# A gate h·cos(h) on one core: the range reduction of the sine without its absolute value

## The chip, the core and the metric

The kernel runs on one core of a Trainium2 chip. The core has a matrix engine (TensorE, PE in the profile), a vector engine (VectorE, DVE), a scalar engine for activation functions (ScalarE, ACT), GpSimd (POOL), and queues that move data by DMA; each has its own stream of instructions and they wait for each other by semaphores. The metric is the device time of one execution in microseconds (us), as the median of several runs.

## The reference

A small attention block makes 4352 rows of 512 numbers; a feed-forward block with a gate follows. All is float32.

```python
def _attn_ref(x, state):          # x (8, 8, 512, 64), state (8, 8, 32, 64)
    scores = scale * np.matmul(x, state.transpose(0, 1, 3, 2))
    ...                           # softmax over the last axis -> a
    xread = np.matmul(a, state)
    scores2 = scale * np.matmul(state, x.transpose(0, 1, 3, 2))
    ...                           # softmax -> a2
    sread = np.matmul(a2, x)
    return np.concatenate([xread, sread], axis=2)

def _moe_ref(x, w_in, w_out):     # x (4352, 512), w_in (512, 2048), w_out (2048, 512)
    h = x @ w_in
    g = h * np.cos(h)
    return g @ w_out
```

The change concerns `g = h * np.cos(h)`.

## The kernel before

The hidden values h are made transposed, in tiles of 128 hidden units by 512 tokens, 16 for each of the 8 batches, and 16 more tiles of 256 columns for the state rows: 144 tiles. The kernel keeps h in turns (h / 2π), so the factor of the sine is 2π. A tile passes five steps after its matmuls: two on ScalarE and one on VectorE that bring the angle into the range of the sine, the sine itself on ScalarE, and the product on VectorE. The constant 12582912 is 1.5·2^23: adding it to a small float32 rounds that to an integer, and subtracting it again gives the integer. The cosine of h turns is then sin(π/2 − 2π·|n − h|), n being that integer; the absolute value keeps the argument between −π/2 and π/2.

```python
MAGIC = 12582912.0
TWO_PI = 2.0 * math.pi
...
msb = ctx.enter_context(tc.tile_pool(name="msb", bufs=2))          # q
hps = ctx.enter_context(tc.tile_pool(name="hps", bufs=2, space=PSUM))  # h
ctx.enter_context(tc.manual_schedule())     # each engine runs in the order written
...
def hidden(t):
    t.hp = hps.tile([P, S], F32, name="h")[:, 0:t.n]
    for i in range(t.kn):
        nc.tensor.matmul(out=t.hp, lhsT=t.lhs(i), rhs=t.rhs(i),
                         start=(i == 0), stop=(i == t.kn - 1))      # L467

def gate(t):
    t.q = msb.tile([P, S], F32, name="q")[:, 0:t.n]
    nc.scalar.activation(t.q, t.hp, func=ACTF.Copy, bias=MAGIC)     # L473

def gate2(t):
    nc.vector.scalar_tensor_tensor(out=t.q, in0=t.q, scalar=MAGIC,  # L476
                                   in1=t.hp, op0=ALU.subtract,
                                   op1=ALU.subtract)

def gate3(t):
    nc.scalar.activation(t.q, t.q, func=ACTF.Abs)                   # L481
    nc.scalar.activation(t.q, t.q, func=ACTF.Sin, bias=halfpi,      # L482
                         scale=-TWO_PI)

def gate4(t):
    t.slot = g_free.pop(0)
    t.g = g_all[:, t.slot, 0:t.n]
    nc.vector.tensor_tensor(t.g, t.hp, t.q, op=ALU.mult)            # L488
```

The loop over the tiles mixes the gate with other work, and that order is the order of each engine:

```python
for step, t in enumerate(all_tiles):
    ...
    hidden(t)
    go(0)                      # PE: parts of the next batch's attention
    gate(t)
    gate2(t)
    go(1); go(3)               # ACT and DVE: parts of the next batch's attention
    convert(last, "bcdf")      # DVE, POOL: weights of an earlier step, bit work
    convert(conv, "1")         # ACT: weights (in some steps after gate4)
    gate3(t)
    later.pop(0)()             # DVE: an output transposed for storing, if there is one
    gate4(t)
    sums(t)                    # DVE or POOL: sums of g tiles
    go(2)
    convert(conv, "2")         # ACT
    go(4)
    ...
    while len(line) >= (LAG if step >= 2 * NH else LAG + 1):
        output(line.pop(0))    # PE: products of g with w_out, LAG = 3 tiles later (L532)
    line.append(t)
```

The weights come in a form whose exponent and mantissa are put together on the chip in parts: `convert` is two passes on ScalarE (L225, L228), two on VectorE (L231, L234) and one on GpSimd (L239) for each piece, in the first 15 steps or so. `products` (L314) multiplies a piece of w_in with a batch's states into `sw`, which ScalarE or VectorE copies to SBUF (L441). The attention's softmax uses the exponential on ScalarE (L355, L360) and a row of VectorE operations (L328 to L381); before the exponentials of a batch, and before the next sine, ScalarE loads another table of functions. `warm` (L709) are matmuls of zeros that keep PE going in the first steps.

## Time and profile before

| | |
|---|---|
| time, median of 3 runs | 787.93 us (786.89 to 788.06) |
| span of the profiled run | 785.0 us |
| PE matmul busy | 765.1 us |
| VectorE busy | 417.3 us |
| ScalarE busy | 389.1 us |
| GpSimd busy | 176.7 us |
| TensorE clock granted | full speed throughout |

The span falls into three stages. In the table each cell is busy time in us in that stage; DMA is the mean share of the 16 DMA engines.

| stage (us from the start) | PE | DVE | ACT | POOL | DMA |
|---|---|---|---|---|---|
| 41 to 103: weights are still converted | 54.46 | 46.23 | 56.98 | 24.31 | 0.64 |
| 103 to 160: last conversions, batch 2 is prepared | 54.17 | 39.24 | 30.88 | 44.65 | 0.20 |
| 160 to 785: steady work, and the state rows at the end | 619.29 | 305.18 | 276.53 | 94.93 | 0.19 |

Busy time counts an instruction from its start to its end. PE's matmuls overlap each other, so a busy PE isn't PE at its peak; the spacing of their starts tells more. In a row of the profile's groups stand the line of the kernel, the engine, the operation, the tile written and the tile read, their shapes, how often, the busy time and the mean time of one, and after the second bar the time for which the engine stood idle just before, with what ended it. L473 means line 473.

### The profile page before, as it was taken

The page shows a single profiled execution, that of the slowest core. Times are in us where ns is not written, and L with a number is a line of the kernel's source. Part 1 is how long each engine was busy: PE and PEld are TensorE (multiplying, and loading weights), DVE is VectorE, ACT ScalarE, POOL GpSimd, SP SyncE. Part 2 cuts the span into 40 slices and gives each one's busy share as a digit, 9 for nine tenths or more (in the row PEclk, how much of TensorE's full clock was granted, in tenths as well). Part 3 has the DMA queues.
Part 4 walks back from the last instruction along what each step waited for, and adds up shares of the span by engine and source line. Part 5 has one row for each costly group of instructions (what it writes and reads, how often), then busy time and mean ns, then how long its engine had stood idle before and what let it go on. Part 6 is the DMA issues. An engine that isn't in the chain of part 4 may idle for free.

```text
span 785.0 us, 7535 instructions
## 1 busy us (share of the span) xinstructions
PE 765.1 (97%) x2664; PEld 340.3 (43%) x2664; DVE 417.3 (53%) x656; ACT 389.1 (50%) x626; POOL 176.7 (23%) x118
## 2 busy tenths in 40 slices
PE   8998899899999999999999999999999999999997
PEld 3443433344344444444344434434444444455554
DVE  5768778623563466734554467635554446431431
ACT  3888954733463545633473446443563445322222
POOL 2344359673000000641000001640000004610200
PEclk9999999999999999999999999999999999999999
DMA  8595451060011510250104310330100114000021
GB/s 241 167 263 187 141 100 28 4 104 1 3 25 31 102 24 5 34 101 0 24 5 76 58 27 15 54 67 0 28 1 0 28 28 130 4 0 15 13 41 40
DMA packets 161957, 43.49 MB, mean 55 GB/s; under 512 B 153920, under 2 KB 153920, under 8 KB 161920
## 3 DMA queue, kind: packets, MB, share of 16 engines
q1 hardware_dynamic: 161024, 42.49, 24.8%
q10 hardware_dynamic: 768, 0.39, 0.2%
q8 instruction: 21, 0.34, 0.2%
q0 software_dynamic: 128, 0.13, 0.1%
q14 instruction: 16, 0.13, 0.1%
HBM read 34.08 MB, written 8.91 MB: 55 GB/s over the span
## 4 chain that ended last, share of the span: by engine, by line
PE 81%; ACT 10%; DVE 6%; issue 1%; DMA 1%; SPq 0%; POOL 0%; DVEq 0%
PE o L532 44%; PE h L467 26%; PE at L314 4%; PE o L652 4%; PE at L404 2%; ACT q L482 1%; ACT q L481 1%; ACT s L228 1%; DVE q L476 1%; ACT q L473 1%; DVE g_all L488 1%; ACT xT L360 1%; ACT w_in L225 1%; ACT L482 1%; DVE xT L334 1%
## 5 line engine op out<-in xcount | busy, mean ns | idle before, releaser
L467 PE MATMUL h<-aT,sw 128*128 128x512 f32 x512 | 241.5, 594 | 11.0 <-DVE g_all L488 8.1
L532 PE MATMUL o<-g_all,w_out 128*128 128x512 f32 x512 | 236.4, 598 | 1.2 <-POOL w_out L239 1.2
L494 POOL TENSOR_TENSOR g_all<-g_all 128x512 f32<-128x512 f32 x80 | 112.1, 1423 | 451.5 <-DVE g_all L488 447.9
L473 ACT ACTIVATE q<-h 128x512 f32<-128x512 f32 (+1 forms) x144 | 82.1, 570 | 262.3 <-PE h L467 262.2
L476 DVE SCALAR_TENSOR_TENSOR q<-q,h 128x512 f32<-128x512 f32 (+1 forms) x144 | 94.2, 654 | 216.9 <-ACT q L473 216.9
L532 PE MATMUL o<-g_all,s 128*128 128x512 f32 x384 | 177.3, 598 | 0.0
L488 DVE TENSOR_TENSOR g_all<-h,q 128x512 f32<-128x512 f32 (+1 forms) x144 | 94.8, 658 | 124.8 <-ACT q L482 118.6
L467 PEld LDWEIGHTS h<-aT,sw 128*128 128x128 f32 x512 | 96.4, 190 | 135.4 <-issue 110.7
L532 PEld LDWEIGHTS o<-g_all,w_out 128*128 128x128 f32 x512 | 94.0, 190 | 125.5 <-issue 118.4
L481 ACT ACTIVATE q<-q 128x512 f32<-128x512 f32 (+1 forms) x144 | 87.6, 608 | 93.5 <-DVE q L476 93.4
L532 PEld LDWEIGHTS o<-g_all,s 128*128 128x128 f32 x384 | 70.8, 190 | 91.7 <-issue 87.3
L482 ACT ACTIVATE q<-q,halfpi 128x512 f32<-128x512 f32 (+1 forms) x144 | 100.5, 698 | 4.5
L239 POOL TENSOR_TENSOR w_out<-w_out,s 128x1024 int32<-128x1024 int32 x10 | 23.9, 2390 | 77.1 <-DVE w_out L234 73.5
L494 DVE TENSOR_TENSOR g_all<-g_all 128x512 f32<-128x512 f32 x48 | 33.2, 692 | 1.6
L441 ACT COPY sw<-at 128x512 f32<-128x512 f32 x50 | 26.8, 589 | 9.0 <-PE at L314 9.0
L467 PE MATMUL h<-sT,w_in 128*128 128x256 f32 x128 | 30.2, 379 | 0.0
L652 PE MATMUL o<-w_out,g_all 128*128 128x512 f32 x64 | 29.6, 592 | 0.0
L467 PEld LDWEIGHTS h<-sT,w_in 128*128 128x128 f32 x128 | 24.3, 190 | 10.1 <-issue 6.7
L239 POOL TENSOR_TENSOR w_in<-w_in,s 128x1024 int32<-128x1024 int32 (+1 forms) x10 | 19.3, 1929 | 38.8 <-DVE w_in L234 36.5
L314 PE MATMUL at<-w_in,stT 64*32 64x512 f32 x400 | 27.2, 601 | 0.0
L538 DVE SCALAR_TENSOR_TENSOR held<-o,held 128x512 f32<-128x512 f32 x40 | 25.3, 675 | 2.9 <-PE o L532 2.9
L559 DVE STREAM_TRANSPOSE ot<-held 128x512 f32<-128x512 f32 x32 | 22.1, 692 | 0.0
(80 smaller groups left out, 427.7 us busy)
## 6 DMA issues: line engine op xcount, KB each, us to landing
out_dram<-ot SPq DMA_DIRECT2D x132, 64.0 KB, 2.0
g_all<-in_moe_w_out_dram SPq DMA_DIRECT2D x8, 1024.0 KB, 4.9
g_all<-in_moe_w_in_dram SPq DMA_DIRECT2D x6, 1024.0 KB, 5.2
xT<-in_x_dram SPq DMA_DIRECT2D x96, 64.0 KB, 2.3
x_b<-in_x_dram SPq DMA_DIRECT2D x24, 256.0 KB, 4.6
x_b<-in_x_dram SPq DMA_DIRECT2D x16, 128.0 KB, 4.0
g_all<-in_moe_w_in_dram SPq DMA_DIRECT2D x4, 512.0 KB, 6.0
x_b<-in_moe_w_out_dram SPq DMA_DIRECT2D x1, 1024.0 KB, 5.9
```

Source lines behind the costliest of these rows:

```text
L239: nc.gpsimd.tensor_tensor(bits, bits, e, op=ALU.add)
L314: nc.tensor.matmul(out=(to or at)[j][Ns * k:Ns * k + Ns, 0:n], lhsT=w[D * j:D * j + D, self.b, Ns * k:Ns * k + Ns], rhs=r(slice(D * j, D * ...
L441: (copy or nc.scalar.copy)(sw_of[self.b, nt][:, j, c0:c1], to[j][:, 0:c1 - c0])
L467: nc.tensor.matmul(out=t.hp, lhsT=t.lhs(i), rhs=t.rhs(i), start=(i == 0), stop=(i == t.kn - 1))
L473: nc.scalar.activation(t.q, t.hp, func=ACTF.Copy, bias=MAGIC)
L476: nc.vector.scalar_tensor_tensor(out=t.q, in0=t.q, scalar=MAGIC, in1=t.hp, op0=ALU.subtract, op1=ALU.subtract)
L481: nc.scalar.activation(t.q, t.q, func=ACTF.Abs)
L482: nc.scalar.activation(t.q, t.q, func=ACTF.Sin, bias=halfpi, scale=-TWO_PI)
L488: nc.vector.tensor_tensor(t.g, t.hp, t.q, op=ALU.mult)
L494: engine.tensor_tensor(out, a, b, op=ALU.subtract)
L532: nc.tensor.matmul(out=acc[bank][ch], lhsT=w[:, i, P * ch:P * ch + P], rhs=g.g, start=(i == 0), stop=(i == NH - 1))
L652: nc.tensor.matmul(out=acc[MAIN][i], lhsT=t.g[:, P * i:P * i + P], rhs=w_out[:, :, t.f, :], start=(t.n_th == 0), stop=(t.n_th == NF - 1))
```

## The change

ScalarE's first pass adds 1/4 instead of the large constant, and writes its result as int32; the conversion to int32 gives the integer n near h + 1/4. VectorE then subtracts h from the integer, reading one int32 and one float operand. Now n − h lies between −1/4 and 3/4, so π/2 − 2π(n − h) lies between −π and π, which the sine takes as it is: no absolute value is needed. Each tile has one ScalarE instruction less, and the sine waits for VectorE directly. The order of the other instructions on each engine stays.

```diff
-MAGIC = 12582912.0
 TWO_PI = 2.0 * math.pi
 ...
     def gate(t):
         t.q = msb.tile([P, S], F32, name="q")[:, 0:t.n]
-        nc.scalar.activation(t.q, t.hp, func=ACTF.Copy, bias=MAGIC)
+        nc.scalar.activation(t.q.bitcast(I32), t.hp, func=ACTF.Copy, bias=0.25)
 
     def gate2(t):
-        nc.vector.scalar_tensor_tensor(out=t.q, in0=t.q, scalar=MAGIC,
-                                       in1=t.hp, op0=ALU.subtract,
-                                       op1=ALU.subtract)
+        nc.vector.tensor_tensor(t.q, t.q.bitcast(I32), t.hp, op=ALU.subtract)
 
     def gate3(t):
-        nc.scalar.activation(t.q, t.q, func=ACTF.Abs)
         nc.scalar.activation(t.q, t.q, func=ACTF.Sin, bias=halfpi,
                              scale=-TWO_PI)
```

## The prediction

> **What bounds the kernel now.** I read the page's busy shares first, then the waits of TensorE (PE), then the groups of instructions by shape, then the chain that ended last, then the timeline around each PE stop.

> ```profile
> PE 765.1 (97%) x2664; PEld 340.3 (43%) x2664; DVE 417.3 (53%) x656; ACT 389.1 (50%) x626; POOL 176.7 (23%) x118
> ```

> PE is the bound over the span; ScalarE (ACT), whose work the change removes, is busy half of it. What ACT gives up can only come back where PE stood still for it. The waits of PE:

> ```profile
> PE h L467 <- DVE g_all L488: 8.1, 7, 1.9
> PE h L467 <- ACT sw L441: 2.9, 2, 2.4
> ...
> PE o L532 <- POOL w_out L239: 1.2, 1, 1.2
> ```

> (us in total, times, longest.) The first is a wait for the last of the gate's five steps: a PSUM buffer h (there are two) is free only when VectorE (DVE) has written g from it. The gate's rows by shape (busy us, mean ns of one, idle before):

> ```profile
> L482 ACT ACTIVATE q<-q,halfpi 128x512 f32<-128x512 f32 x128 | 92.4, 722 | 4.0
> L481 ACT ACTIVATE q<-q 128x512 f32<-128x512 f32 x128 | 80.9, 632 | 86.6 <-DVE q L476 86.6
> L473 ACT ACTIVATE q<-h 128x512 f32<-128x512 f32 x128 | 76.0, 594 | 206.0 <-PE h L467 205.9
> L488 DVE TENSOR_TENSOR g_all<-h,q 128x512 f32<-128x512 f32 x128 | 88.0, 688 | 113.8 <-ACT q L482 107.6 <-issue 5.3 <-POOL g_all L494 0.4
> L476 DVE SCALAR_TENSOR_TENSOR q<-q,h 128x512 f32<-128x512 f32 x128 | 87.4, 683 | 171.7 <-ACT q L473 171.7
> ```

> L481 is the absolute value that goes. In the whole span its 87.5 us (with 16 narrow ones of 415 ns) lie mostly beside PE. But between 41 and 103 us, where the weights are still converted, the chain runs along ACT without a stop (start, us, what):

> ```profile
> 44.54 1.03 ACT s L228
> 45.57 0.49 ACT q L473
> 46.06 0.02 issue
> 46.08 0.70 DVE q L476
> 46.78 0.02 issue
> 46.80 0.64 ACT q L481
> 47.44 0.03 issue
> 47.47 0.72 ACT q L482
> 48.19 1.07 ACT w_in L225
> 49.26 1.05 ACT s L228
> ```

> The period is about 4.8 us a tile there, and PE's own work in it is nearly as long, so few stops appear. After about 103 us the chain is PE with short exceptions. To size the stops I take a full-width matmul in a stream as 0.43 us (the chain has 1.72 us for four), and compare where a group should end with where the next starts. The starts of the restarts, with what ended the idle time:

> ```profile
> 32.94 1.99 PE L467 MATMUL h<-aT,sw 128*128 128x512 f32 x4 [0.66 <-DVE g_all L488]
> 45.13 1.98 PE L532 MATMUL o<-g_all,w_out 128*128 128x512 f32 x4 [1.16 <-POOL w_out L239]
> 76.10 1.98 PE L467 MATMUL h<-aT,sw 128*128 128x512 f32 x4 [1.95 <-DVE g_all L488]
> 83.45 1.98 PE L467 MATMUL h<-aT,sw 128*128 128x512 f32 x4 [2.43 <-ACT sw L441]
> 102.99 1.98 PE L467 MATMUL h<-aT,sw 128*128 128x512 f32 x4 [1.21 <-DVE g_all L488]
> 146.14 1.98 PE L467 MATMUL h<-aT,sw 128*128 128x512 f32 x4 [1.86 <-DVE g_all L488]
> ```

> At 76.10, for instance, four matmuls began at 72.27 and needed 1.72, so PE was free at 73.99 and lost 2.11. In this way I get lost: 0.87 at 32.94, 1.33 at 45.13, 0.70 at 54.55 (transposes that wait for an ACT copy), 0.44 at 59.9 (a wait for DVE), 2.11 at 76.10, 2.60 at 83.45, 1.36 at 102.99, 2.02 at 146.14, 1.13 at 151.69, and 0.87 and 0.86 at 322.76 and 493.83. Together 14.3 us: the most that any relief of ACT can give.

> [...] busy rows say PE lost 20 us in all, the start-to-start spacing shows more inside the same stops (2.11 against 1.95). [...] a row of this kernel, the ACT pass L228 that turns uint32 into int32, takes 1148 ns for 1024 elements beside 1165 for the float pass L225. [...] I take int32 minus float from PSUM to cost what L488, the same form in float, costs. No row before shows the mixed form.

> **The change part by part.** *First pass*: the float pass with the bias 12582912 becomes the same pass with 0.25 and an int32 output: 594 ns stays. *Second pass*: scalar_tensor_tensor at 683 becomes tensor_tensor at about 688: 128 × 5 ns, under 1 us over the span and off the path. *Third pass*: 144 absolute values go, 87.5 us of ACT. Where ACT is the chain, one is worth 0.67 us (46.80 to 47.47). *Order*: the other instructions keep their order on each engine; the sine now waits for DVE itself. Where a table load stands between (8 times) it no longer comes after the absolute value, which waited for DVE, and runs beside the DVE pass: at 142.6 to 144.65 the sine can then start some 1.4 us earlier.

> On the path I move each event by what its latest input allows:
> - To 45.13. One absolute value before 28 us (0.54) gives PE 0.35 at 32.94, since a DVE copy that waits for PE comes between. With the next (30.46) the conversion whose products PE needs at 39.5 comes earlier, another 0.4; with the third (35.85) DVE and POOL deliver w_out 1.65 earlier in all. PE follows: 1.65.
> - To 61. ACT gains 0.67 a tile at 43, 47, 52 and 57; PE can use only its stops at 54.55 and 59.9: 0.70 + 0.35 = 1.05, the sum 2.7.
> - 76.10. The g it waits for comes at the end of a row of DVE instructions (66.1 to 76.0) without idle time. Absolute values don't stand in it: 0 more.
> - 83.45. ACT: 0.67 for the value at 72.22 and 0.53 for that at 78.75. Sum 3.9; +1.2.
> - 102.99. Three more values (83.90, 89.13, 94.41) bring the gate 1.5 to 2 us further; PE can use its stop, 1.35. Sum 5.25.
> - 146.14. The gate's start at 141.36 is set by PE. Behind it the sine gains 1.4, but DVE still has a reciprocal to finish (144.5), so g gains 1.0. At 151.69 all lies on DVE, which moves along: 0 more. Sum 6.25.
> - 322.76 and 493.83: the same turn of a batch; g gains about 1.0, the stops are 0.87 and 0.86: 1.7. Sum 7.95.
> - The end: PE runs from 494 to 780.7 with no such stop, then a copy and the stores. 0.

> 787.93 − 7.95 = 779.98; I say 780.0.

> **The rivals.** (1) *ACT is hidden everywhere*: PE's real work fills 41 to 103, and the stops there are DVE's. Speaks for it: 97% busy, and the stop at 76.10, which is DVE's. Against it: the stop at 83.45 ends with an ACT copy after an unbroken ACT chain. It would leave 785 to 788. (2) *A dearer conversion*: an int32 output or a mixed DVE input takes longer than the float form. If the DVE pass cost 0.3 us more, its 12 or so instances in the weight stage would eat most of the gain: 783 to 788. [...] (3) *All stops go*: with ACT free earlier, conversions, DVE and POOL follow and PE closes every stop: 787.93 − 14.3 = 773.6. Against it: the stops at 76.10 and 151.69 follow rows of DVE instructions without gaps, and those two alone are 3.2 us of the 14.3. (4) *A transfer becomes the bound*: DMA is at 0.73 of its time from 39 to 78 us, so the weights might not land sooner. The waits show ACT waiting 1.1 us for DMA only once, at the start, and a load issued at 48.69 lands some 5 us later while its user starts at 58.08: slack of about 4 us, more than the 2.7 gained by then.

> **Range and chances.** 776.8 to 784.5: below, the DVE rows shrink as well and half of the rest of 14.3 comes; above, half of the gain is lost to rivals 1 or 2. Faster by over 2% needs less than 772.2, below even rival 3: 0.01. Slower by over 2% needs over 803.7, a conversion twice as dear on the path of every tile: 0.02. Within 2%: 0.97.

> **What would show it.** Right: ACT busy near 302 us and 144 instructions fewer; the first pass at 590 to 610 ns and the second at 680 to 695; PE's waits for g down from 8.1 to about 4 us, the largest left the one near 73 (1.9), the stop that was at 83.45 about 1.4 long, none left at 322 and 494; sines with a table load begin straight after it; the end of the weight stage (102.99) about 5 us earlier and the last matmul about 8. Wrong: a first or second pass over 750 ns; the stop near 76 gone, which would say ACT set it; a wait of ACT for DMA in the weight stage; or a change at the end that isn't the sum of the stops closed.

## The result and the profile after

The changed kernel takes 778.83 us (median of 5 runs, 777.93 to 779.22), the kernel before on the same chip 787.76 us: a ratio of 0.9887 with a 95% interval of 0.9872 to 0.9901. That is 8.9 us less, where the prediction had 7.9, and inside its range.

The busy line of the changed kernel's page:

```profile
PE 764.3 (98%) x2664; PEld 340.7 (44%) x2664; DVE 416.6 (54%) x656; ACT 304.1 (39%) x482; POOL 176.4 (23%) x118
```

ScalarE has 144 instructions and 85 us less; its table loads are 16 of 1283 ns as before, so none went with the absolute value. TensorE (PE) does the same work in a shorter span. Its waits (us in total, times, longest):

```profile
PE h L465 <- DVE g_all L484: 3.3, 3, 1.9
...
PE o L267 <- DMA x_b<-in_x_dram: 1.4, 2, 0.8
PE h L465 <- ACT sw L439: 0.5, 1, 0.5
...
PE o L528 <- POOL w_out L237: 0.4, 1, 0.4
```

The wait for g fell from 8.1 to 3.3 us, that for sw from 2.9 to 0.5, that for GpSimd from 1.2 to 0.4. So 8.0 us of the gain lie in waits of PE that stood in three different rows, none of which names the pass that was removed. The gate's rows by shape:

```profile
L478 ACT ACTIVATE q<-q,halfpi 128x512 f32<-128x512 f32 x128 | 92.6, 724 | 76.3 <-DVE q L475 76.2
L472 ACT ACTIVATE q<-h 128x512 int32<-128x512 f32 x128 | 76.2, 595 | 283.2 <-PE h L465 283.1
...
L475 DVE TENSOR_TENSOR q<-q,h 128x512 f32<-128x512 int32 x128 | 87.6, 684 | 220.4 <-ACT q L472 220.3
L484 DVE TENSOR_TENSOR g_all<-h,q 128x512 f32<-128x512 f32 x128 | 87.3, 682 | 53.2 <-ACT q L478 51.7 <-issue 1.3
```

The pass with an int32 output takes 595 ns, the float one took 594. The subtraction with one int32 operand takes 684 ns, the float form took 683. The conversion costs nothing that can be seen in these rows. The sine takes 724 ns with arguments from −π to π, and took 722 from −π/2 to π/2. The starts at which PE still comes back from a stop, after 30 us:

```profile
33.07 1.98 PE L465 MATMUL h<-aT,sw 128*128 128x512 f32 x4 [0.42 <-DVE g_all L484]
43.97 1.98 PE L528 MATMUL o<-g_all,w_out 128*128 128x512 f32 x4 [0.36 <-POOL w_out L237]
73.78 2.85 PE L465 MATMUL h<-aT,sw 128*128 128x512 f32 x4 [1.94 <-DVE g_all L484]
144.76 1.98 PE L465 MATMUL h<-aT,sw 128*128 128x512 f32 x4 [0.96 <-DVE g_all L484]
```

Eleven stops have become four, and the two that end a row of VectorE (DVE) work, at 73.78 and 144.76, are as long as they were (1.95 and 0.97 before). Two of the stops of the kernel before, the one that stayed and one that closed:

```profile
151.69 1.98 PE L467 MATMUL h<-aT,sw 128*128 128x512 f32 x4 [0.97 <-DVE g_all L488]
...
322.76 1.98 PE L467 MATMUL h<-aT,sw 128*128 128x512 f32 x4 [0.71 <-DVE g_all L488]
```

The four matmuls at 73.78 took 2.85 us instead of 1.98: from 74.76 us on PE ran at half its clock for 3.41 us. More of that below.

### The profile page after: what moved, and what is told of

It is laid out like the page before. It is cut to its first block, busy times and chain, and to the rows that moved or that the text cites. A ratio compares the mean times of both kernels' runs of the same rounds, so it can differ in the third digit from the quotient of the medians.

```text
span 776.2 us, 7529 instructions
## 1 busy us (share of the span) xinstructions
PE 764.3 (98%) x2664; PEld 340.7 (44%) x2664; DVE 416.6 (54%) x656; ACT 304.1 (39%) x482; POOL 176.4 (23%) x118
## 4 chain that ended last, share of the span: by engine, by line
PE 91%; DVE 4%; ACT 2%; DMA 1%; issue 1%; POOL 0%; SPq 0%; ACTq 0%; POOLq 0%
PE o L528 49%; PE h L465 30%; PE at L312 4%; PE o L648 4%; PE at L402 2%; PE o L312 1%; PE at L385 1%; DVE xT L332 1%; DMA x_b<-in_x_dram 1%; DVE q L475 1%; DVE i L326 0%; DVE aT L349 0%; DVE g_all L484 0%; ACT q L472 0%; PE o L705 0%
## 5 line engine op out<-in xcount | busy, mean ns | idle before, releaser
L475 DVE TENSOR_TENSOR q<-q,h 128x512 f32<-128x512 int32 (+1 forms) x144 | 94.3, 655 | 271.4 <-ACT q L472 271.4
L472 ACT ACTIVATE q<-h 128x512 int32<-128x512 f32 (+1 forms) x144 | 82.3, 572 | 347.0 <-PE h L465 346.8
L332 DVE STREAM_TRANSPOSE xT<-i 128x1024 f32<-128x1024 f32 x16 | 19.8, 1236 | 0.0
```

The lines of the kernel that those rows point to most:

```text
L332: nc.vector.transpose(out=self.spread.rearrange("p j (t i) -> p (j t) i", i=32), in_=self.m1.rearrange("p j t -> p (j t)").unsqueeze(2) .t ...
L472: nc.scalar.activation(t.q.bitcast(I32), t.hp, func=ACTF.Copy, bias=0.25)
L475: nc.vector.tensor_tensor(t.q, t.q.bitcast(I32), t.hp, op=ALU.subtract)
```

## The experiments

Each run was timed beside the kernel before on the same chip (787.2 to 787.3 us in all three groups). In the diffs `-` and `+` are against the changed kernel.

### e1: the absolute value back, the new forms kept

```diff
     def gate3(t):
+        nc.scalar.activation(t.q, t.q, func=ACTF.Abs)
         nc.scalar.activation(t.q, t.q, func=ACTF.Sin, bias=halfpi,
```

> The changed kernel with the absolute value put back into every tile, ahead of the sine (the cosine is even, so the output stays the same); the int32 pass and the mixed subtraction stay. Theory (what helps is one ScalarE pass less in each tile): all of the gain goes, 786.8 to 788.6 us, and the stops of TensorE at 83 and 146 us are back. Rival (the new forms of the first two passes bring part of it): under 785 us. Rival (the new forms cost something): over 789 us.

Measured: 787.51 us, 1.0002 of the kernel before (0.9994 to 1.0010). Its waits and two of its restarts:

```profile
PE h L465 <- DVE g_all L485: 8.1, 7, 1.9
```

```profile
146.35 1.98 PE L465 MATMUL h<-aT,sw 128*128 128x512 f32 x4 [1.86 <-DVE g_all L485]
...
322.97 1.98 PE L465 MATMUL h<-aT,sw 128*128 128x512 f32 x4 [0.70 <-DVE g_all L485]
```

They are those of the kernel before (1.86 and 0.71). So the gain is the missing pass, to within the 0.8 us of the interval; both rivals about the new forms fall.

### e2 and e3: the absolute value in the first 16 tiles alone, and in all others alone

```diff
     def gate3(t):
+        if t.step < 16:       # e2; in e3: t.step >= 16
+            nc.scalar.activation(t.q, t.q, func=ACTF.Abs)
         nc.scalar.activation(t.q, t.q, func=ACTF.Sin, bias=halfpi,
 ...
     for step, t in enumerate(all_tiles):
+        t.step = step
```

> The absolute value back in the 16 tiles of the first batch alone, where the weights are converted; the other 128 tiles go without. Theory (a sum of stops: 5.2 us of the 8.9 come in the first 103 us, the rest at the turns of the batches near 146, 322 and 494 us): 783 to 785 us, that is about 3.9 below the kernel before. Rival (each of the 144 passes counts alike): 16/144 of the gain lost, 779.8 us. Rival (all of it comes from the weight stage): 787 us or more.

> The converse: the absolute value back in the 128 tiles after the first batch, none in the first 16. Theory: 782 to 783.5 us, about 5 below the kernel before, with the stops near 146, 322 and 494 us of the span back. Together with the run before, the two gains should add up to about 8.9 us. Rival (each pass counts alike): 128/144 of the gain lost, 786.8 us. Rival (all from the weight stage): 779 us.

Measured: e2 783.32 us, ratio 0.9952 (0.9939 to 0.9964), so 4.0 us gained; e3 782.83 us, 0.9942 (0.9928 to 0.9956), so 4.5 us gained. The two gains together are 8.5, against 8.9 for both parts at once. Restarts of e2, with the pass in the weight stage alone:

```profile
103.47 1.98 PE L465 MATMUL h<-aT,sw 128*128 128x512 f32 x4 [1.19 <-DVE g_all L486]
...
150.13 1.98 PE L465 MATMUL h<-aT,sw 128*128 128x512 f32 x4 [0.99 <-DVE g_all L486]
```

The stop at the end of the weight stage is back, while those of 146, 322 and 494 us are gone. In e3 it is the other way round:

```profile
80.09 1.98 PE L465 MATMUL h<-aT,sw 128*128 128x512 f32 x4 [1.23 <-ACT sw L439]
...
141.31 2.91 PE L465 MATMUL h<-aT,sw 128*128 128x512 f32 x4 [1.86 <-DVE g_all L486]
318.37 1.98 PE L465 MATMUL h<-aT,sw 128*128 128x512 f32 x4 [0.70 <-DVE g_all L486]
...
489.44 1.98 PE L465 MATMUL h<-aT,sw 128*128 128x512 f32 x4 [0.71 <-DVE g_all L486]
```

16 passes of 144 carry half of the gain, and the rest comes at three turns of a batch (the stretches that end at the stops near 146, 322 and 494 us, each begun by a new batch's exponentials). The passes don't count alike: most of the 144 lie beside PE's work and cost nothing.

### e4: the load of the sine's table waits for VectorE again

```diff
         getattr(attn[b], name)(*args)
+        if name == "exps":
+            turned_to_exp[0] = True
 ...
+    turned_to_exp = [True]
+
     def gate3(t):
+        if turned_to_exp.pop():       # the 8 sines behind a table load
+            nc.scalar.activation(t.q[:, 0:1], t.q[:, 0:1], func=ACTF.Abs)
+        turned_to_exp.append(False)
         nc.scalar.activation(t.q, t.q, func=ACTF.Sin, bias=halfpi,
```

> The changed kernel, with an absolute value of one single column ahead of the 8 sines that follow a load of the sine's table; so the load waits for VectorE as it did before, but ScalarE is not made to do a full pass. Theory (the ScalarE pass and its place in the chain carry the gain, the overlap of load and VectorE little): 779 to 780.3 us; the sine after a load begins about 0.9 us later than in the changed kernel and only the stop near 146 us opens by 0.2 to 0.6. Rival (the overlap of the table load carries the turns of the batches): the stops near 139, 315 and 486 us open by about 0.9 each, 781.5 us or more.

Measured: 778.79 us, 0.9889 (0.9876 to 0.9903): the same as the changed kernel, and 0.2 us below the range. In the profile the load begins at 136.81 us, behind the short pass that waited for VectorE, and the sine comes 2.86 us after the start of the tile's first pass, where the changed kernel has 1.90: later by the 0.9 us that were meant. Its restarts:

```profile
79.82 1.98 PE L467 MATMUL h<-aT,sw 128*128 128x512 f32 x4 [1.32 <-ACT sw L439]
...
139.60 1.98 PE L467 MATMUL h<-aT,sw 128*128 128x512 f32 x4 [0.42 <-DVE g_all L491]
145.15 1.98 PE L467 MATMUL h<-aT,sw 128*128 128x512 f32 x4 [0.97 <-DVE g_all L491]
```

The stop near 139 opens by 0.42 and those near 315 and 486 stay shut, as the theory said; counted from the start of the first hidden tile, the last matmul starts 0.6 us later than in the changed kernel's profile (750.1 against 749.5), which the medians don't resolve. The overlap of the load is a small part of the gain.

### e9: a pass of the same size, but not in the tile's chain

```diff
     nc.vector.memset(zeros, 0.0)
+    spare = consts.tile([P, S], mybir.dt.bfloat16)
+    nc.gpsimd.memset(spare, 0.0)
 ...
         nc.scalar.activation(t.q, t.q, func=ACTF.Sin, bias=halfpi,
                              scale=-TWO_PI)
+        nc.scalar.activation(spare[:, 0:t.n], spare[:, 0:t.n], func=ACTF.Abs)
```

> The changed kernel with a ScalarE pass of the same size behind the sine of each tile, on a spare tile that nothing else reads: it takes ScalarE's time as the absolute value did, but doesn't stand between the subtraction and the sine. Theory (in the weight stage ScalarE's time counts, since its work is one unbroken chain there; at the turns of the batches the length of the gate's own chain counts): the first 103 us lose nearly all of their gain, the turns near 146, 315 and 486 us lose 0.6 us together, 783 to 785 us. Rival (only the shorter chain of a tile counts): 779 to 780 us. Rival (only ScalarE's time counts, everywhere): 787 us or more.

Measured: 783.66 us, 0.9950 (0.9938 to 0.9963). The pass itself, and the restarts from 80 to 145 us:

```profile
L482 ACT ACTIVATE spare<-spare 128x512 bf16<-128x512 bf16 x128 | 78.9, 616 | 0.0
```

```profile
83.02 1.98 PE L467 MATMUL h<-aT,sw 128*128 128x512 f32 x4 [2.27 <-ACT sw L441]
102.03 1.98 PE L467 MATMUL h<-aT,sw 128*128 128x512 f32 x4 [0.67 <-DVE g_all L487]
143.58 1.98 PE L467 MATMUL h<-aT,sw 128*128 128x512 f32 x4 [0.26 <-DVE g_all L487]
```

In the weight stage most of the gain is lost again: PE is back at 102.03, where the kernel before has 102.99 and the changed one 98.23. Counted from the first hidden tile, 1.3 of the 5.2 us are left. There ScalarE's time counts, for the most part wherever in the tile it is spent. At the turn near 146, 0.26 of the stop is left where the kernel before had 1.86: there it is mainly the length of the gate's own chain. The 0.26 is ScalarE's time here too, for the spare pass also stands ahead of the exponentials: the gate's first pass of that tile starts 1.33 us after the matmuls of the next hidden tile start (1.89 in the kernel before, 0.87 in the changed one). Both rivals fall; each is mainly right in one stage.

### e5, e6, e7, e8: what holds the stops that are left

e5 moves the DVE part of the conversion in tile 9 behind that tile's product; e6 also moves a ScalarE conversion pass of tile 10 behind the copy of sw in tile 11; e7 gives six DVE copies of batch 1 to ScalarE; e8 is all three.

```diff
 # e5 (and e6, e8)
-            elif last >= 0:
+            elif last >= 0 and step != 9:
                 convert(last, "bcdf")
 ...
         gate4(t)
+        if step == 9:
+            convert(last, "bcdf")
 # e6 (and e8)
             go(1)
+            if step == 11:
+                convert(last, "2")
             go(3)
 ...
-        if conv >= 0:
+        if conv >= 0 and step != 10:
             convert(conv, "2")
 # e7 (and e8)
-            if b == 1 and nt > 0:
+            if False:
                 x_dve[s].append((b, "products_taken", nt) + bank)
```

> The changed kernel, with the VectorE part of one weight conversion (tile 9) moved behind that tile's product g, out of the row of VectorE work that ends the longest stop left, 1.94 us before 73.78. Theory (behind that row ScalarE's own row sets the next event: exponentials, table load, sine, the copy of sw that TensorE waits for near 80 us): the stop at 73.78 closes to under 0.3 us, but TensorE then stands still before the copy of sw, so 778 to 779 us, less than 0.8 gained. Rival (VectorE's row alone sets it): 776.5 to 777.3 us.

Measured: 779.07 us (777.54 to 779.42), ratio 0.9885 (0.9867 to 0.9902); nothing gained in the median. The restart:

```profile
79.82 3.13 PE L465 MATMUL h<-aT,sw 128*128 128x512 f32 x4 [2.58 <-ACT sw L439]
```

The stop near 73 is gone, and the wait stands one tile later and is 2.58 us long. Behind DVE's row lay ScalarE's. Of the four executions the three with a mean clock of 0.997 took 778.83 to 779.42, the one with 0.999 took 777.54, so the median also holds a slower clock, of which more below.

> The same, and the second ScalarE pass of the next weight conversion (1.07 us) moved behind the copy of sw, so that the sw TensorE waits for comes earlier. Theory: sw and the g it also needs are there about 1.2 us earlier, near 78.7 us, 777.0 to 777.9 us in all. Rival (the stops there are set by something else, such as a transfer or GpSimd): as the run before.

Measured: 777.47 us, 0.9871 (0.9856 to 0.9885). Its restarts:

```profile
78.99 1.98 PE L465 MATMUL h<-aT,sw 128*128 128x512 f32 x4 [1.55 <-ACT sw L439]
84.08 1.98 PE L465 MATMUL h<-aT,sw 128*128 128x512 f32 x4 [0.51 <-DVE g_all L484]
```

sw comes earlier as said, but a tile later a new stop of 0.51 takes half of that back. By the profile (from the start of the first hidden tile to that of the last matmul 749.2 us, 749.5 in the changed kernel) only 0.3 us is won; the rest of the lower median isn't explained by these stops.

> The changed kernel, with the six copies of sw in batch 1 that VectorE made (677 ns each) given to ScalarE, which has room now. Theory (the stop at 144.76, 0.96 us by the page and 1.1 by the spacing of starts, ends a row of VectorE work with two of these copies in it): the stop closes, 777.4 to 778.1 us. Rival (ScalarE's later sine takes the place of the wait): 778.5 us or more.

Measured: 776.33 us, 0.9861 (0.9846 to 0.9877). No stop is left after these two:

```profile
73.48 1.98 PE L465 MATMUL h<-aT,sw 128*128 128x512 f32 x4 [1.95 <-DVE g_all L484]
79.61 1.98 PE L465 MATMUL h<-aT,sw 128*128 128x512 f32 x4 [1.22 <-ACT sw L439]
```

The one at 144.76 has closed: 1.3 us by the profile (748.2 against 749.5), close to the expected 1.1. The median gained more than that, 2.5, and lies 1.1 below the range; executions of one kernel lie up to 2.8 us apart (e3), and why the median gained so much is open.

> All three moves on the changed kernel. Theory (the stops are separate and add up): 775.8 to 776.8 us, with no stop of TensorE over 0.6 us after 50 us. Rival (closing one stop opens another): 777.5 us or more.

Measured: 776.31 us (776.08 to 776.62), 0.9856 (0.9842 to 0.9871): the range holds and the reason only in part. The stops before 78.98 (1.55) and 84.07 (0.51) are those of e6, so the claim that none over 0.6 would be left was wrong, and e8 is no faster than e7 alone. e7 and e8 are faster than both kernels; against the changed one this goes by the ratios to the kernel before, whose intervals lie apart for e8 and overlap a little for e7 (changed kernel 0.9872 to 0.9901).

### e10 and e11: the long stop filled with matmuls

```diff
+        if step == 11:
+            warm(2, acc[SIDE][1])     # zeros; four matmuls in the profile
         if step != 1:
             hidden(t)
```

e10 is this on the changed kernel, e11 on e7.

> The changed kernel with four matmuls of zeros put ahead of the hidden tile that waits near 73.78 us, to fill the longest stop of TensorE that is left (2.1 us by the spacing of starts) to about 0.4. Their output is read by nothing. Theory (the 3.4 us at half clock that the profiles show about 1 us after a stop of 1.9 us or more follow from the stop): no such piece in the profile and a mean clock of 0.999 or more in every execution; the time stays at 778.2 to 778.9 us, as the next stop, near 80 us, is the longer for it. Rival (the half clock comes from something else): clocks of 0.995 to 0.997 in most executions as before.

Measured: 777.78 us, 0.9878 (0.9865 to 0.9892), 0.4 us below the range; clocks of 0.999 in three executions and 0.998 in one, where the theory wanted 0.999 in each. The changed kernel had 0.995 to 0.997 in three of five. Its restarts:

```profile
73.68 1.98 PE L465 MATMUL h<-aT,sw 128*128 128x512 f32 x4 [0.27 <-DVE g_all L484]
79.80 1.98 PE L465 MATMUL h<-aT,sw 128*128 128x512 f32 x4 [1.20 <-ACT sw L439]
```

The stretch behind the stop, in the changed kernel and in e10 (busy us of PE, its weight loads, DVE, ScalarE and GpSimd, then the granted PE clock and DMA):

```profile
74.70:78.30 3.60, 3.60 (x19) 0.53 (x17) 2.82 (x6) 3.57 (x5) 0.93 (x1) 0.53 0.76 283
```

```profile
74.70:78.30 3.60, 3.60 (x23) 1.00 (x21) 2.96 (x6) 3.57 (x4) 0.84 (x1) 1.00 0.72 278
```

Clock 0.53 in the one, 1.00 in the other. The stop near 80 appears in e10 because PE arrives there in time to wait.

> The six copies of sw of batch 1 on ScalarE, as in e7, and the stop near 73.78 us filled with matmuls of zeros. Theory: no half clock, and the executions of e7 that took 1.6 us more are gone: 776.0 to 776.6 us in all of them. Rival (the slow executions come from elsewhere): some at 778 us again.

Measured: 776.73 us (776.18 to 777.13), 0.9862 (0.9847 to 0.9878). No execution at 778 came, as one of e7's four had been, but three of four lie above the 776.6 that was expected; the fill is no gain over e7.

## Why the prediction was right, step by step

The table counts how much earlier PE reaches each event than before, in the sum of the steps so far. 0.44 us is added to each measured shift, because the first hidden tile started at 21.72 instead of 21.28: x came later (the wait for x_b was 0.8 us and is 1.4), which differs from profile to profile (21.3 to 22.0) and isn't the change.

| event before -> after (us) | predicted sum | measured sum |
|---|---|---|
| 45.13 -> 43.97 | 1.65 | 1.60 |
| 76.10 -> 73.78 | 2.7 | 2.76 |
| 83.45 -> 80.16 | 3.9 | 3.73 |
| 102.99 -> 98.23 | 5.25 | 5.20 |
| 146.14 -> 139.26 | 6.25 | 7.32 |
| 151.69 -> 144.76 | 6.25 | 7.37 |
| tile 143 (state rows), 771.95 -> 763.07 | 7.95 | 9.32 |

Without the 0.44 us the last row is 8.9, the difference of the medians. The first four steps hold within 0.2 us: the chain through DVE and GpSimd to 45, the cap by PE's own stops up to 61, nothing at 76.10 since DVE's row sets it (in e5, with a part of that row moved, the stop is gone), 1.2 and then 1.35 more from ScalarE. e9 and e2 show that this stage is bought mostly with ScalarE's time.

The term that was mis-sized is the one at 146.14: 1.0 predicted, 2.1 measured. There I wrote that the gate's start at 141.36 was set by PE. It was not. PE's start of the next hidden tile and the row of ScalarE around it in the kernel before, and then in the changed one:

```profile
139.47 1.88 PE L467 MATMUL h<-aT,sw 128*128 128x512 f32 x4
```

```profile
136.37 0.63 ACT L481 ACTIVATE q<-q 128x512 f32<-128x512 f32 x1 [1.25 <-DVE q L476]
137.03 0.72 ACT L482 ACTIVATE q<-q,halfpi 128x512 f32<-128x512 f32 x1
...
141.36 0.59 ACT L473 ACTIVATE q<-h 128x512 f32<-128x512 f32 x1
142.70 0.63 ACT L481 ACTIVATE q<-q 128x512 f32<-128x512 f32 x1 [0.75 <-DVE q L476]
143.35 1.28 ACT L482 ACT_TABLE_LOAD   x1
144.65 0.72 ACT L482 ACTIVATE q<-q,halfpi 128x512 f32<-128x512 f32 x1
```

```profile
134.61 1.88 PE L465 MATMUL h<-aT,sw 128*128 128x512 f32 x4
```

```profile
131.16 0.72 ACT L478 ACTIVATE q<-q,halfpi 128x512 f32<-128x512 f32 x1 [0.84 <-DVE q L475]
...
135.48 0.59 ACT L472 ACTIVATE q<-h 128x512 int32<-128x512 f32 x1
136.09 1.28 ACT L478 ACT_TABLE_LOAD   x1
137.38 0.72 ACT L478 ACTIVATE q<-q,halfpi 128x512 f32<-128x512 f32 x1
```

```profile
138.26 0.37 DVE L369 RECIPROCAL i<-i 128x34 f32<-128x34 f32 x1
138.54 0.63 DVE L484 TENSOR_TENSOR g_all<-h,q 128x512 f32<-128x512 f32 x1
```

The line of 141.36 names no wait: the pass follows the exponentials at once, and the matmuls that ended at 141.35 made the next tile's h, not this one's. So the absolute values ahead of the exponentials count too: the sine ahead of them starts 5.87 us earlier (137.03 to 131.16) and the gate 5.88, PE at the same point only 4.86 (139.47 to 134.61), which is 1.0. Of this, 0.66 is the absolute value at 136.37 itself, and the rest that of the tile before, for whose sine DVE waited 0.30 us at 133.86. From the gate to g the other 1.0 comes as I had it: the load (136.09, 1.28 us) runs beside DVE's pass (136.10, 0.69 us), and g follows DVE's reciprocal at once (138.54; 145.40 before). The stop closes altogether.

At 151.69 nothing was predicted and 0.05 came. The stops at 322.76 and 493.83 closed as said; they gave 0.98 and 0.97 and not 0.87 and 0.86, since four matmuls after a stop take 0.1 us more than four in a stream (1.98 against 1.88), which my sizing left out. The end kept its share.

Of the signs named, one read otherwise: the stop near 83 was to be 1.4 us long and is missing. e4 and e10 show it, 1.32 and 1.20 long, where PE kept its clock. In the changed kernel's profile PE loses 1.6 us to the half clock just before (6.38 us from 73.78 to 80.16 with no stop; before, 7.35 from 76.10 to 83.45 less a stop of 2.60 makes 4.75), and so reaches that place late enough not to wait. Counted from the first hidden tile it gets there 58.44 us later, in e7, without the half clock, 58.22: the loss that stays is 0.2 us. The dearer conversion is refuted by the two rows and e1, the hidden ScalarE by e3, where the first 16 tiles alone bring 4.5 us, and by e2, and the transfer by ScalarE's waits for DMA, still one of 0.9 us at the start.

## What to carry to other kernels

To price work taken from an engine that isn't the bound, list the bound engine's stops by the spacing of its starts, follow each back through every engine to the pass in question, and cap each gain by the stop: here 87.5 us of ScalarE work was worth 8.9. The stop that ends an unbroken row on another engine didn't move here (1.95 us before, 1.94 after), and closing it alone only passed the wait on to the next row (2.58 us in e5). Look whether the profile names a wait before an instruction, and for which tile the supposed releaser works, before calling the instruction held by it: the line that named none was the term that was mis-sized.

## What the runs showed of the hardware that was not expected

In e3's profile the piece followed the stop of 1.86 before 141.31, whose four matmuls took 2.91 us. Where such stops are gone or filled (e6, e8, e10, e11), 16 executions had mean clocks of 0.998 to 1.000; two of them had 0.998, which is also what e3's profile has with its piece, so these two don't exclude one. The kernel before had 0.997 or less in 11 of the 17 executions beside e1 to e4. e10 differs from the changed kernel by the fill alone and points the same way; with four and five executions it is not proof. What the piece costs depends on what follows: all but 0.2 us is swallowed by the next stop in the changed kernel; in e5, where no stop followed, it costs 1.7 us (66.40 us from 79.82 to the stop near 146, 64.70 in e10).
